# Delta-rule attention ahead of two mixtures: one matmul pass that reads the state for k and q together

## The chip, the cores and the metric

One core of a Trainium2 chip runs the whole program. The metric is the time of one execution in microseconds on the device, the median of several runs. The engines, by their names in the profile: TensorE (PE, with PEld for its weight loads), VectorE (DVE), ScalarE (ACT), GpSimd (POOL), and SyncE (SP), which issues the transfers.

## What is computed

```python
B, H, S, D = q.shape                      # 4, 8, 768, 48
k_n = k / (norm(k) + 1e-06)
state = zeros((B, H, D, D))
for t in range(S):
    y[:, :, t] = einsum('bhd,bhde->bhe', q[:, :, t], state)
    v_old = einsum('bhde,bhd->bhe', state, kt)
    state = state + bt * einsum('bhd,bhe->bhde', kt, vt - v_old)
x = y.transpose(0, 2, 1, 3).reshape(B * S, H * D)      # 3072 x 384
x = (silu(x @ w_gate) * (x @ w_val)) @ w_out           # d_ff 1536
h = x @ w_in                                           # d_ff 2048
out = (h * tanh(softplus(h))) @ w_out2
```

A token's q reads the state before that token changes it, and so does its k.

## The kernel before

The 768 positions are cut into chunks of C = 32, and three chunks (NCH) make a step of 96, so there are 24 chunks in 8 steps. The four batches stand side by side in the 128 partitions, 32 each. Inside a chunk the recurrence is solved in closed form: with the products of the chunk's k (`gram`), a triangular system is inverted on VectorE for a whole step at once (`inverse`, lines 333 and 340, 31 pairs of instructions that shrink and grow, ending in the transposition of line 343), and the rest is matmuls, three steps of work per chunk (`chain`):

1. `read` with w = 0 (tile ks, 16 matmuls of 128 rows and 32 columns, 96 columns moving): k times the state of the chunks before. VectorE subtracts it from v (line 371). Next to it stands `gram_pair` of a later chunk (32 matmuls of 48x32, evacuated by two copies on ScalarE into g and two masked products on VectorE into p).
2. `att_solved` (z, 32 matmuls of 32x32): the inverse times v; ScalarE copies it out in two masked versions.
3. `read` with w = 1 (tile y): q times the state; `att_out` adds p times z into the same tile and ScalarE copies y out in one instruction (line 402); `att_update` (ds, 16 matmuls of 64x48) makes the change of the state, which VectorE adds in four instructions (line 434).

The state lies as a [128, B, NP, 2, D] tile: of two heads one in partitions 0 to 47 and one in 64 to 111, each in its own columns and zeros in the others, so that one matmul of 128 rows handles two heads of one batch. k and q of a chunk come transposed and padded from the host (`kqT`, five buffers, 4 KB a partition: first the k of the four batches, then their q), one transfer per chunk; v and k also come in natural layout.

Between these blocks runs the first mixture for the step before: `mix1(t)` has 36 groups of nine matmuls of 128x128 on 384 columns (`gate`, `val`, `down`, 12 times), each about 1.56 us. In `val` VectorE multiplies the silu with the product (h, line 720), ScalarE and GpSimd split it in two parts (hp), and `down` takes them two groups later. `three` and `down` call `tick` after each third of a group, and `tick` runs what is due in the list `ev`. The list is made by `plan` in units of groups: `BEGIN`, `STEADY`, `LAST` and `CHAIN` place the three parts of each chunk, `GRAM2`, `GRAM`, `NEXT` and `EARLY1` the grams and inversions. Attention step t runs beside mixture step t-1; step 0 of attention and its set-up run before, in the order written out in `START`. Each engine takes its instructions in the order in which they were written.

PSUM has eight banks: psa has two that rotate (tag a, through `bank`: gram, ds, y, xt) and one (tag y, through `odd`: ks, z, ds), psm has one each for g, v and the three x2 of the mixture. In `START` free banks of psm are lent out.

Beside all this the weights of both mixtures are converted from 64-bit floats (`conv_begin`, `conv_step`, `conv_tail`: two instructions on ScalarE, one on VectorE, then a split or a store to w2d); the second mixture (from about 649 us) is not touched by the change.

## Time and profile before

| | us |
|---|---|
| median of 3 runs | 1058.05 |
| lowest and highest | 1056.12 and 1058.16 |
| span of the profiled execution | 1055.1 |
| own time of the profiled execution | not listed apart from the three runs |
| TensorE busy | 1025.4 |
| VectorE busy | 514.3 |
| ScalarE busy | 399.6 |
| GpSimd busy | 189.3 |

The span is from the first to the last instruction. Busy time of TensorE is modelled and overlaps between instructions, so a full TensorE is not one at its peak; how long a block of matmuls takes is read from the chain, in which one block follows the other. A matmul on 32-bit floats has two records in the trace, so 16 matmuls show as x32.

### The profile page before, as it was taken

How to read it: one execution, taken by the hardware profiler on the slowest of the kernel's cores; microseconds unless marked ns; L12 is line 12 of the kernel's file. 1: busy time of each engine (PE TensorE's matmuls, PEld its weight loads, DVE VectorE, ACT ScalarE, POOL GpSimd, SP SyncE). 2: the span in 40 equal slices, each digit the busy share in tenths (PEclk: the TensorE clock that was granted, in tenths of full speed). 3: DMA queues.
4: the chain of work that ended last, by engine and by line, in shares of the span. 5: the costliest groups of instructions: out<-in, count | busy, mean ns of one | idle time of the engine just before them, and what ended most of it. 6: DMA issues, size and time to landing. Idle time of an engine off the chain costs nothing.

```text
span 1055.1 us, 28813 instructions
## 1 busy us (share of the span) xinstructions
PE 1025.4 (97%) x12691; PEld 981.9 (93%) x12691; DVE 514.3 (49%) x1117; ACT 399.6 (38%) x877; POOL 189.3 (18%) x212
## 2 busy tenths in 40 slices
PE   6799989999999999999999999999999999999998
PEld 5689889989999999999999999999999999999998
DVE  7666994895775966857831343222222221212111
ACT  3568644234243243342322445333323233323232
POOL 2576631312213113212121111000000000000000
PEclk7799999999999999999999999999999999999999
DMA  8156524115124133140010143000001010100000
GB/s 305 30 188 213 176 98 149 62 56 157 65 83 147 38 123 107 44 148 26 31 47 2 61 151 98 23 23 23 31 16 37 9 39 7 46 1 31 1 23 23
DMA packets 37709, 77.48 MB, mean 73 GB/s; under 512 B 4176, under 2 KB 23760, under 8 KB 37584
## 3 DMA queue, kind: packets, MB, share of 16 engines
q1 hardware_dynamic: 37584, 75.65, 22.0%
q8 instruction: 99, 1.62, 0.6%
q14 instruction: 26, 0.21, 0.1%
HBM read 59.90 MB, written 15.73 MB: 72 GB/s over the span
## 4 chain that ended last, share of the span: by engine, by line
PE 85%; DVE 9%; issue 2%; ACT 1%; DMA 1%; POOL 1%; SPq 1%; DVEq 0%; ACTq 0%; POOLq 0%
PE o L669 19%; PE h L669 19%; PE v L669 12%; PE g L669 11%; PE x L741 11%; DVE t_tmp L333 3%; DVE t_sys L340 2%; PE z L379 2%; PE ds L417 2%; PE ks L359 2%; PE gram L465 2%; PE y L393 1%; PE y L359 1%; DVE h L720 1%; DVE state L434 1%
## 5 line engine op out<-in xcount | busy, mean ns | idle before, releaser
L1026 DVE TENSOR_TENSOR gl<-gg,gh 128x384 fp32r<-128x384 f32 x128 | 71.4, 558 | 319.2 <-ACT gh L1025 319.2
L726 POOL TENSOR_TENSOR hp<-h,hp 128x384 fp32r<-128x384 f32 x96 | 100.0, 1042 | 416.7 <-ACT hp L725 408.4
L1020 ACT ACTIVATE gg<-h 128x384 f32<-128x384 f32 x128 | 62.9, 492 | 264.8 <-PE h L669 264.8
L741 PE MATMUL x<-hp,w1h 128*128 128x384 f32 x576 | 132.3, 339 | 4.0 <-ACT w1h L623 2.1
L669 PE MATMUL o<-w2l,gh 128*128 128x384 f32 x384 | 129.4, 337 | 0.0
L669 PE MATMUL o<-w2h,gh 128*128 128x384 f32 x384 | 129.2, 336 | 0.0
L669 PE MATMUL o<-w2h,gl 128*128 128x384 f32 x384 | 129.2, 336 | 0.0
L725 ACT CAST hp<-h 128x384 fp32r<-128x384 f32 x96 | 49.2, 513 | 179.7 <-DVE h L720 179.6
L741 PEld LDWEIGHTS x<-hp,w1h 128*128 128x128 f32 x576 | 101.6, 188 | 6.6 <-ACT hp L725 2.5
L669 PE MATMUL h<-x2h,w2h 128*128 128x384 f32 x384 | 88.0, 337 | 0.0
L669 PE MATMUL h<-x2l,w2h 128*128 128x384 f32 x384 | 87.8, 336 | 0.0
L669 PE MATMUL h<-x2h,w2l 128*128 128x384 f32 x384 | 87.7, 336 | 0.0
L720 DVE TENSOR_TENSOR h<-s,v 128x384 f32<-128x384 f32 x96 | 52.8, 550 | 66.7 <-PE v L669 65.1
L333 DVE TENSOR_TENSOR t_tmp<-t_sys,g_sys 128x31 f32<-128x31 f32 (+15 forms) x186 | 81.0, 435 | 4.6
L340 DVE TENSOR_TENSOR t_sys<-t_sys,t_tmp 128x31 f32<-128x31 f32 (+15 forms) x186 | 75.7, 407 | 6.4
L712 ACT ACTIVATE s<-g 128x384 f32<-128x384 f32 x96 | 47.1, 491 | 77.7 <-PE g L669 77.5
L434 DVE TENSOR_TENSOR state<-state,ds 48x384 f32<-48x384 f32 x92 | 47.0, 549 | 58.1 <-PE ds L417 57.6
L669 PEld LDWEIGHTS o<-w2h,gl 128*128 128x128 f32 x384 | 72.1, 188 | 0.0
L669 PEld LDWEIGHTS o<-w2h,gh 128*128 128x128 f32 x384 | 72.1, 188 | 0.0
L669 PEld LDWEIGHTS o<-w2l,gh 128*128 128x128 f32 x384 | 72.1, 188 | 0.0
L669 PE MATMUL v<-xh,w1h 128*128 128x384 f32 x288 | 66.8, 339 | 4.9 <-DVE h L720 4.9
L669 PEld LDWEIGHTS h<-x2h,w2h 128*128 128x128 f32 x384 | 68.9, 188 | 0.0
(128 smaller groups left out, 1775.8 us busy)
## 6 DMA issues: line engine op xcount, KB each, us to landing
raw<-in_w_first_dram SPq DMA_DIRECT2D x36, 384.0 KB, 3.7
raw<-in_w_second_dram SPq DMA_DIRECT2D x32, 384.0 KB, 3.6
kqT<-in_kq_dram SPq DMA_DIRECT2D x23, 512.0 KB, 4.7
w2d<-f SPq DMA_DIRECT2D x32, 192.0 KB, 3.6
w2raw<-w2d SPq DMA_DIRECT2D x16, 384.0 KB, 3.0
v<-in_v_dram SPq DMA_DIRECT2D x24, 192.0 KB, 3.1
x2d<-xs SPq DMA_DIRECT2D x24, 192.0 KB, 1.8
x2raw<-x2d SPq DMA_DIRECT2D x24, 192.0 KB, 2.4
```

The costliest lines, as they stand in the source:

```text
L333: nc.vector.tensor_tensor(out=tmp, in0=t_sys[:, 0:m, j:j + 1].to_broadcast([128, m, n]), in1=g_sys[:, j:j + 1, j + 1:C].to_broadcast([128, ...
L340: nc.vector.tensor_tensor(out=sl, in0=sl, in1=tmp, op=ALU.subtract)
L359: nc.tensor.matmul(out=ps[bs, 2 * p:2 * p + 2], lhsT=kqt[:, p, w, bs], rhs=state[:, b, p], start=not w or p == 0, stop=not w, skip_group_c ...
L434: nc.vector.tensor_tensor(out=st, in0=st, in1=pss[x][rows], op=ALU.add)
L669: nc.tensor.matmul(out=ps, lhsT=a, rhs=b, start=start and i == 0, stop=stop and i == len(seq) - 1)
L712: nc.scalar.activation(out=s, in_=ps, func=AF.Silu)
L720: nc.vector.tensor_tensor(out=h, in0=g_t.pop(j), in1=ps, op=ALU.mult)
L725: nc.scalar.copy(out=hh, in_=h)
L726: nc.gpsimd.tensor_tensor(out=hl, in0=h, in1=hh, op=ALU.subtract)
L741: nc.tensor.matmul(out=x2[kk], lhsT=w[j][:, 6 + kk, :], rhs=m, start=j == 0 and i == 0, stop=j == J1 - 1 and i == 2,)
L1020: nc.scalar.activation(out=gg, in_=ps, func=AF.Mish)
L1026: nc.vector.tensor_tensor(out=gl, in0=gg, in1=gh, op=ALU.subtract)
```

## The change

For steps 1 to 7 (step 0 keeps the old `read` and `att_out`):

- `read_both` takes the place of both reads. For each pair of heads, batch and half of the rows, one matmul with 48 rows of weights and 64 columns: 32 columns of k and 32 of q of one batch, laid side by side; 48 columns of the state move. Its tile `both` has two banks and stays held until the output is copied. k's result falls into the partitions of its own batch b, q's into those of the neighbour b^1. VectorE takes k's part off v with two masked multiply-adds (`less_of` is -1 in the partitions of even or odd batches and 0 elsewhere) in place of one subtraction.
- `out_both` adds p times z onto q's part, in the neighbour's partitions, and ScalarE copies y out in four instructions of 32 partitions.
- kq is laid down as k0 q0 q1 k1 k2 q2 q3 k3, for chunks 3 and later with four transfers of 256- and 128-byte pieces (chunks 0 to 2 keep the old layout and `k_at`, `kq_at` know both). v is laid down with even heads ahead of odd ones, in two transfers of 192-byte pieces, and is read so everywhere (`by_parity`). kq of a chunk is now loaded again right after `read_both`, not after the output.
- The two rotating banks become the halves of `both` (`half`). While `both` is held, gram's and the update's tiles lie in bank v of the mixture (`free_v`) and in bank y.
- The plan's numbers: each chunk has a place (`SPOTS`, `STEADY`), with its parts 1.5 groups (steps 1 and 2, `SOON`) or 3 groups apart (`EVEN`); `GRAM2` and two entries of `EARLY1` are new. The state's update is added first for the batches whose bank is v.

```diff
+    def load_kq(n):
...
+            if n < NCH:
+                nc.sync.dma_start(out=kq_of(n), in_=kq[n])
+                return
+            to = kq_of(n).rearrange("r p w f -> r p (w f)")
+            nc.sync.dma_start(
+                out=to.rearrange("r p (x f) -> r p x f", x=2)[:, :, :, C:3 * C],
+                in_=kq[n][:, :, 1].rearrange("r p (x f) -> r p x f", x=2),
+            )
+            nc.sync.dma_start(out=to[:, :, 3 * C:5 * C], in_=kq[n][:, :, 0, C:3 * C])
+            nc.sync.dma_start(out=to[:, :, 0:C], in_=kq[n][:, :, 0, 0:C])
+            nc.sync.dma_start(out=to[:, :, 7 * C:8 * C], in_=kq[n][:, :, 0, 3 * C:4 * C])
...
+    both = psa.tile([128, 2, 512], F32, tag="both", name="both", bufs=1)
+    read_of = both[:, :, 0:2 * NP * D].rearrange("q w (x p d) -> q w x p d", x=2, d=D)
...
+    @phased
+    def read_both(t, c):
+        held.append(c)
+        for p in range(NP):
+            for b in range(B):
+                cols = slice(64 * (b // 2), 64 * (b // 2) + 64)
+                for par in range(2):
+                    rows = slice(64 * par, 64 * par + D)
+                    nc.tensor.matmul(
+                        out=read_of[cols, par, b % 2, p],
+                        lhsT=both_at(num(t, c), rows, p, b),
+                        rhs=state[rows, b, p, par],
...
+        load_kq(num(t, c) + 5)
+        yield
+        vv = v_s[c].rearrange("q (w p) d -> q w (p d)", w=2)
+        for x in range(2):
+            nc.vector.scalar_tensor_tensor(
+                out=vv, in0=read_of[:, :, x].rearrange("q w p d -> q w (p d)"), scalar=less_of[:, x:x + 1], in1=vv, op0=ALU.mult, op1=ALU.add
+            )
...
+    def out_both(t, c):
+        for h in range(H):
+            for b in range(B):
+                bs = slice(C * b, C * b + C)
+                to = slice(C * (b ^ 1), C * (b ^ 1) + C)
+                nc.tensor.matmul(
+                    out=read_of[to, h % 2, b % 2, h // 2],
+                    lhsT=p_nat[num(t, c) % 5][bs, h, :],
+                    rhs=z_s[bs, b % 2, h, :],
...
+        held.clear()
+        for b in range(B):
+            nc.scalar.copy(
+                out=y_s[c][C * b:C * b + C].rearrange("q (p w d) -> q w p d", w=2, d=D),
+                in_=read_of[C * (b ^ 1):C * (b ^ 1) + C, :, b % 2],
+            )
...
-        pss = [bank([128, NP, 2, C], "gram") for _ in range(2)]
+        if held:
+            pss = [f([128, NP, 2, C], "gram") for f in (free_v, odd)]
+        else:
+            pss = [bank([128, NP, 2, C], "gram") for _ in range(2)]
...
-            pss = [f([128, NP, 2, D], "ds") for f in (bank, odd)]
+            pss = [f([128, NP, 2, D], "ds") for f in (free_v, odd)]
```

On TensorE, around the output of a steady chunk (third chunk of attention step 3, beside mixture step 2, both counted from 0). Before, with the reads apart:

```order
L359 MATMUL ks<-state,kqT_102 32x96 x16
L465 MATMUL gram<-kqT_101 32x64 x32
L669 MATMUL v<-xh,w1h_2185 128x384 x3
L669 MATMUL v<-xh,w1l_2186 128x384 x3
L669 MATMUL v<-xl,w1h_2185 128x384 x3
```

```order
L669 MATMUL g<-xh,w1h_2461 128x384 x3
L359 MATMUL y<-state,kqT_102 32x96 x16
L393 MATMUL y<-z_s,p_107 32x48 x32
L417 MATMUL ds<-z_s,k_97 48x96 x16
L669 MATMUL g<-xh,w1l_2462 128x384 x3
L669 MATMUL g<-xl,w1h_2461 128x384 x3
```

And the same two places now:

```order
L439 MATMUL both<-state,kqT_103 64x48 x32
L574 MATMUL gram<-kqT_102 32x64 x32
L775 MATMUL g<-xh,w1h_2188 128x384 x3
L775 MATMUL g<-xh,w1l_2189 128x384 x3
L775 MATMUL g<-xl,w1h_2188 128x384 x3
```

```order
L847 MATMUL x_3996<-hp,w1h_2188 128x384
L461 MATMUL both<-z_s,p_108 32x48 x32
L523 MATMUL ds<-z_s,k_98 48x96 x16
L775 MATMUL g<-xh,w1h_2426 128x384 x3
L775 MATMUL g<-xh,w1l_2427 128x384 x3
```

The read of y has left the second place, and both places have moved from inside a gate to the end of a down, ahead of a whole gate. (x is the result of a down, g and v those of a gate and a val.)

On VectorE, at the start of attention step 5. Before, the transposition that ends the inversion stands ahead of h:

```order
L333 TENSOR_TENSOR t_tmp<-t_sys,g_sys 128x112
L340 TENSOR_TENSOR t_sys<-t_sys,t_tmp 128x28x4
L720 TENSOR_TENSOR h<-s,v 128x384
L333 TENSOR_TENSOR t_tmp<-t_sys,g_sys 128x87
...
L343 STREAM_TRANSPOSE t_nat<-t_sys 128x32x32
L720 TENSOR_TENSOR h<-s,v 128x384
L371 TENSOR_TENSOR v_98<-v_98,ks 128x384
L481 TENSOR_TENSOR p_110<-gram,mask 128x4x32 x2
```

Now:

```order
L826 TENSOR_TENSOR h<-s,v 128x384
L388 TENSOR_TENSOR t_tmp<-t_sys,g_sys 128x112
...
L395 TENSOR_TENSOR t_sys<-t_sys,t_tmp 128x31
L826 TENSOR_TENSOR h<-s,v 128x384
L398 STREAM_TRANSPOSE t_nat<-t_sys 128x32x32
L710 SCALAR_TENSOR_TENSOR f<-raw 128x384
L451 SCALAR_TENSOR_TENSOR v_99<-both,less_of,v_99 128x384 x2
L590 TENSOR_TENSOR p_111<-gram,mask 128x4x32 x2
```

The second h has moved ahead of the transposition, one pair of the inversion (112) behind the first h, a conversion (f) ahead of the read's result, and there are two instructions on v where there was one.

On SyncE's queue at the start of the program, behind the loads of k, of kq 0 to 2 and of beta. Before:

```order
L159 DMA v_98<-in_v_dram 128x384
L159 DMA v_99<-in_v_dram 128x384
L159 DMA v_100<-in_v_dram 128x384
L166 DMA kqT_104<-in_kq_dram 128x1024
L166 DMA kqT_105<-in_kq_dram 128x1024
L166 DMA kqT_101<-in_kq_dram 128x1024
```

Now:

```order
L160 DMA v_101<-in_v_dram 128x4x48 x2
L176 DMA kqT_105<-in_kq_dram 128x8x64
L180 DMA kqT_105<-in_kq_dram 128x4x64
L181 DMA kqT_105<-in_kq_dram 128x4x32
L182 DMA kqT_105<-in_kq_dram 128x4x32
```

Each load of v is two transfers and each of kq 3 to 5 (the last ones ahead of the first weights) four.

## Rows read from the trace of the kernel before

**Rows 1.** The page: span, and busy time and share of two engines.
```profile
span 1055.1 us, 28813 instructions
PE 1025.4 (97%) x12691; PEld 981.9 (93%) x12691; DVE 514.3 (49%) x1117; ACT 399.6 (38%) x877; POOL 189.3 (18%) x212
```

**Rows 2.** Busy time by stage; the first row names the columns.
```profile
core 0: us, PE busy (x) PEld busy (x) DVE busy (x) ACT busy (x) POOL busy (x), PEclk, DMA share, GB/s
...
56.00:147.00 91.00, 84.49 (x1709) 76.13 (x1709) 73.63 (x136) 61.28 (x140) 57.41 (x54) 0.98 0.54 175
...
386.80:461.08 74.28, 73.91 (x1198) 69.25 (x1198) 53.87 (x127) 26.23 (x57) 17.52 (x16) 1.00 0.30 96
```

**Rows 3.** Who waited for whom: total us, times, longest us.
```profile
ACT raw L593 <- DMA raw<-in_w_second_dram: 19.3, 9, 3.1
...
PE v L669 <- DVE h L720: 4.9, 7, 2.0
```

**Rows 4.** The chain through one steady step: start us, us, what.
```profile
400.57 0.80 PE ks L359 x32
401.37 0.79 PE gram L465 x53
402.15 1.76 PE g L669 x9
...
406.52 0.81 PE z L379 x64
...
411.72 0.80 PE y L359 x32
412.52 0.81 PE y L393 x64
413.33 0.81 PE ds L417 x32
```

**Rows 5.** Weight loads by form: count, busy us, mean ns, idle before.
```profile
L741 PEld LDWEIGHTS x<-hp,w1h 128*128 128x128 f32 x576 | 101.6, 188 | 6.6 <-ACT hp L725 2.5 <-ACT w1h L623 2.5
...
L465 PEld LDWEIGHTS gram<-kqT 48*32 48x32 f32 x1536 | 17.7, 111 | 6.1 <-issue 2.6 <-DMA kqT<-in_kq_dram 0.6 <-ACT p L479 0.2
```

**Rows 6.** Timeline at a step's start: start us, us, instruction, [idle before].
```profile
446.28 0.38 DVE L333 TENSOR_TENSOR t_tmp<-t_sys,g_sys 128x220 f32<-128x220 f32 x1
...
446.72 0.69 PE L669 MATMUL g<-xh,w1h 128*128 128x384 f32 x3
...
451.94 0.79 PE L669 MATMUL v<-xh,w1h 128*128 128x384 f32 x3 [0.37 <-DVE h L720]
...
454.13 2.14 DVE L343 STREAM_TRANSPOSE t_nat<-t_sys 128x1024 f32<-128x1024 f32 x1
...
456.58 0.56 DVE L371 TENSOR_TENSOR v<-v,ks 128x384 f32<-128x384 f32 x1
...
457.55 0.54 DVE L481 TENSOR_TENSOR p<-gram,mask 128x128 f32<-128x128 f32 x2 [0.41 <-ACT g_nat L476]
```

**Rows 7.** ScalarE: output copies of one step; one full stretch of step 1.
```profile
L402 ACT COPY y<-y 128x384 f32<-128x384 f32 x3 | 1.4, 479 | 3.6 <-PE y L393 3.6
...
80.00:86.00 6.00, 6.00 (x149) 5.41 (x148) 3.05 (x5) 6.00 (x15) 3.98 (x5) 1.00 0.78 235
```

**Rows 8.** The DMA queue at 447 to 456 (x2d) and 16 to 22 us (raw).
```profile
q1 hardware_dynamic: 432, 0.59, 17.7%
...
q1 hardware_dynamic: 864, 2.37, 101.7%
```

**Rows 9.** The start: SyncE's issues of kq 3 to 5, landings, gram of kq 5.
```profile
6.61 2.03 SPq L166 DMA_DIRECT2D kqT<-in_kq_dram  x3
...
DMA to landing us min/median/max: 5.6/7.8/8.7
...
22.10 0.89 PE L465 MATMUL gram<-kqT 48*32 48x32 f32 x64
```

More of the change, by code (lines that the diff above doesn't have):

```diff
@@ L196, in tile_delta_attention_moe_moe, with half @@
     starting = [0]
+    both = psa.tile([128, 2, 512], F32, tag="both", name="both", bufs=1)
+    read_of = both[:, :, 0:2 * NP * D].rearrange("q w (x p d) -> q w x p d", x=2, d=D)
+    turns = [0]
+    held = []
+    def half(shape):
+        turns[0] += 1
+        n = 1
+        for x in shape[1:]:
+            n *= x
+        flat = both[:, turns[0] % 2, 0:n]
+        if len(shape) == 2:
+            return flat
+        names = "abc"[:len(shape) - 1]
+        return flat.rearrange(
+            f"p ({' '.join(names)}) -> p {' '.join(names)}", **dict(zip(names, shape[1:]))
+        )
     def bank(shape, name):
@@ L347, in read @@
         if w:
-            if starting and c == 1:
+            if c == 1:
                 hold["y"] = psm.tile([128, H, D], F32, tag="x21", name="y")
             else:
-                hold["y"] = psa.tile([128, H, D], F32, tag="y", name="y", bufs=1) if starting else bank([128, H, D], "y")
+                hold["y"] = psa.tile([128, H, D], F32, tag="y", name="y", bufs=1)
         if t == 0 and c == 0:
@@ L424, in att_update @@
         yield
[L425 to L435 removed]
+        for i in range(4):
+            par, x = (i // 2, i % 2) if starting else (i % 2, i // 2)
+            rows = slice(64 * par, 64 * par + D)
+            st = state[rows, 2 * x:2 * x + 2, :, par].rearrange("q b p d -> q p b d")
+            if n == 0 and x:
+                nc.scalar.copy(out=st, in_=pss[x][rows])
+            elif n == 0:
+                nc.vector.tensor_copy(out=st, in_=pss[x][rows])
+            else:
+                nc.vector.tensor_tensor(out=st, in0=st, in1=pss[x][rows], op=ALU.add)
+            if i == 1 and not starting:
                 yield
@@ L510, in chain, with last_of @@
     def chain(t, c):
-        hold = {}
         return [
-            lambda: (read(t, c, 0, hold), [gram_pair(*x) for x in with_read(t, c)]),
+            lambda: (read_both(t, c), [gram_pair(*x) for x in with_read(t, c)]),
             lambda: att_solved(t, c),
-            lambda: (read(t, c, 1, hold), att_out(t, c, hold), later(att_update.begin(t, c))),
+            lambda: last_of(out_both.begin(t, c), att_update.begin(t, c)),
         ]
-    def later(update):
+    def last_of(output, update):
+        next(output)
         next(update)
         next(update)
-        ev.append((now[0] + 0.9 if begun[0] < n_prep else now[0], lambda: next(update, None)))
+        ev.append((now[0] + (1.9 if begun[0] < n_prep else 0.0), lambda: next(update, None)))
+        for i in range(B):
+            ev.append((now[0] + 1.2 + 0.3 * i, lambda: next(output, None)))
         ev.sort(key=lambda e: e[0])
@@ L533, in plan @@
     def plan():
[L534 to L535 removed]
+        spots = {t: [GROUPS * (t - 1) + x for x in SPOTS.get(t, STEADY)] for t in range(1, NST)}
+        begin = {t: x[0] for t, x in spots.items()}
         def when(t, c, i):
@@ L860, in heat_on @@
     def heat_on(n):
[L861 removed]
+        ps = half([128, N])
         for _ in range(n):
```

100 lines of the change are left out of this document (60 added, 40 removed).

## The prediction

> **What bounds the kernel now.** I read the page first: TensorE is busy for 1025.4 of 1055.1 us, VectorE for half [rows 1]. Then the stages [rows 2]: a step in the steady state, 386.80 to 461.08 us, has TensorE busy for 73.91 of 74.28 us, while step 0 of the mixture with attention step 1 (56 to 147 us) leaves 6.5 us idle and has VectorE and ScalarE busy too. Then the waits [rows 3]: between TensorE and everything else only 4.9 us in seven waits go to the product h of the mixture. So from 56 us on what counts is time on TensorE, and a microsecond less of it there is a microsecond less of the whole, until another engine or a buffer makes TensorE wait. Last the chain inside a steady step [rows 4], which prices every attention block of a chunk: ks 0.80, gram 0.79, z 0.81, y from the state 0.80, y from z 0.81, ds 0.81 us.
>
> **Part 1, the reads, what the change is for.** Per chunk of steps 1 to 7 (21 chunks) the two reads, 0.80 + 0.80 = 1.60 us [rows 4], go, and one read_both of 32 matmuls comes. Its price R is not in the trace. ks has 32 records of 96 columns, z 64 of 48, ds 32 of 96: 3072 columns each, always over four tiles (128x32, 32x32, 64x48), and each takes 0.80 to 0.81 us. read_both has 64 records of 48 columns, 3072 again, over four tiles of 64x64: R = 0.81 if all four run together. It walks the tiles in pairs, though (the two row halves twice, then the other column half), and loads weights of 64 columns, where no burst here has more than 48. The upper bound from rows: gram makes 64 loads of 32 columns in 0.79 us; if those loads set its time, twice the columns cost 1.58. Two tiles at a time instead of four give twice 0.81 = 1.62. I take R = 0.85, close to ds, which is nearest in form (half the rows, four tiles, every second record in the other half). Saving 0.75 x 21 = 15.75 us; the ends are 0.79 x 21 = 16.6 and nothing. The output block keeps 32 matmuls of 32x32 and ds its 16, in one burst as before.
>
> The rows on weight loads show mean latencies of 111 ns for 32 columns and 188 ns for 128 [rows 5], 0.80 ns a column. The Trainium skill ("TensorE: Matmul & The Clock Gate", sections "LDWEIGHTS (loading the stationary operand)" and "The mechanism") gives columns / 1.2 ns per load and lets a load pass a running matmul only if their row groups differ. Taken strictly, read_both's 32 loads of 64 columns in each row half would need 32 x 53 = 1.71 us, and the sum would have a loss of 0.11 x 21 = 2.3 us here instead of a gain. The trace speaks against it: ks' 32 loads in the same rows would need 0.85 us by it and took 0.80 with everything. It is a rival below.
>
> **Part 2, VectorE.** The one subtraction (0.56 us, [rows 6]) becomes two masked multiply-adds of the same size: 0.56 x 3 = 1.7 us a step more, on an engine with 20 us idle in a steady step [rows 2]. Over most of the step that is hidden. It isn't at the step's start, and there lies the new wait: gram now stands in bank v, which the next val needs, so val waits until VectorE has multiplied gram's first half by the mask. Row by row from 446.28 [rows 6]: eleven pairs of solve to 454.13 less one h, 7.3; two h, 1.1; the back transposition 2.1; one f, 0.6; two multiply-adds 1.15; half of p 0.3: 12.5 us, so 458.8. TensorE from its gate at 446.72: five groups of 1.56, read 0.85, gram 0.80, gate 1.76 behind a burst [rows 4]: val is ready at 457.9. Wait 0.9 us. The wait of 0.37 in the place before [rows 6] partly goes, as the solve's end is 0.8 group later and one pair stands behind the earlier h. Net 0.6 x 6 step starts (steps 2 to 7) = 3.6 us; bounds -2 (VectorE one pair earlier, and the present waits go) and 6 x 2.5 = 15 (late by a transposition more). ds in bank v instead of its own costs nothing: the two adds that free v come first, 0.1 + 2 x 0.55 = 1.2 us, under the gate of 1.76 that follows; without that cover it would be 21 x 1.2 us.
>
> **Part 3, ScalarE.** One output copy of 0.48 us [rows 7] becomes four over 32 partitions. Priced like the whole one (its length is the same, only partitions differ) that is 1.44 us more per chunk. In a steady step ScalarE has 48 us idle [rows 2] and three of the four stand before a gate's silu, which comes 0.81 + 1.76 us after the output block: hidden. In step 1 it is not idle: 6.00 of 6 us at 80 to 86 [rows 7]. 3 x 1.44 = 4.3 us at worst, 0 at best; I take 1.0, a quarter of it, since over the stage it is idle for a third of the time (61.28 of 91 us, [rows 2]).
>
> **Part 4, the transfers.** kq goes from 128 rows of 4 KB to 2560 pieces of 256 and 128 bytes in four transfers, v from 128 rows to 1024 of 192 bytes in two. No such piece is in the trace. Two rows give a price by size [rows 8]: the writes of x2d, 1536 bytes, 0.177 x 9 us x 16 engines / 432 = 59 ns a packet (with the small completion packets counted), the raw weights of 3072 bytes, 1.017 x 6 x 16 / 864 = 113 ns. Time follows bytes, and the line through both ends near 5 ns at zero (150 at 4 KB), so some 10 to 15 ns for these pieces; the other end is 59, as if size made no difference. I take 20, nearer the line since halving the bytes nearly halved the time. In the steady state this is hidden: a kq is first read by gram one chunk, nine groups, over 14 us of matmuls, after its load, and 2560 x 20 / 16 = 3.2 us of transfer fits. The raw weights of w_second queue behind it on SP, and ScalarE waits for those already (19.3 us in nine waits, up to 3.1, [rows 3]) without a wait of TensorE on it: no price, but up to 2 us for each of the nine if that cover is gone.
>
> It is not hidden at the start. There three v and kq 3 to 5 are loaded in a row while the transfers run without a gap; kq 5 is issued by 8.6 us and lands 8.7 us later, at about 16.9; its gram runs at 22.10, followed on ScalarE by the first weight conversions and then the first join [rows 9]. Slack 5.2 us. New: 3 x (1024 + 2560) = 10752 pieces x 20 / 16 = 13.4 us, less the old 384 rows of 1536 bytes and 384 of 4 KB, (384 x 59 + 384 x 150) / 16 = 5.0: 8.4 us later, 3.2 of it past the slack. Bounds: at 12 ns 3.1 us, inside the slack, so 0; at 59 ns 39.6 - 5.0 - 5.2 = 29 us.
>
> **Part 5, the moved steps.** Chains start at groups 4.8, 13.8, 22.8 with a step of 3 groups instead of 2.5, all whole blocks at the end of a down; steps 1 and 2 have 1.5 groups between read and z, about 2.1 us of TensorE work over a need of 0.1 + 1.15. The solve of step 2 gets 30.6 groups instead of 28.1, which helps the fullest stretch of VectorE about as much as the extra multiply-adds and the tighter spacing take there. Zero, with +-2 in the range.
>
> **Sum.** -15.75 + 3.6 + 1.0 + 3.2 = -7.95 us. The profiled execution has a span of 1055.1; its own total isn't listed, so I set it level with the median, 2.95 around the span. Against the span: 1047.2; against the median of the three runs, 1058.05 - 7.95 = **1050.1**.
>
> **The rivals.**
> (a) As summed: 1050.1.
> (b) The covers hold everywhere: no wait at bank v (VectorE a pair earlier), small pieces near the line: -16.6 + 0.5 = 1042. For it: only 4.9 us of waits for h now; against: VectorE has no gap before the read from 446.28 to the end of its subtraction [rows 6].
> (c) The read is not cheaper: two tiles at a time or loads that bind, R = 1.6, no saving: 1058.05 + 7.8 = 1065.9, slower. For it: the order in pairs, 64 columns; against: ds alternates halves too and reaches four tiles' pace. The skill's strict rule is the same mechanism with 1.71: 1058.05 + 2.3 + 7.8 = 1068.
> (d) Small pieces cost as the row of 1536 bytes does: the start is late by 10 to 29 us, 1057 to 1076. This alone turns the sign from about 32 ns a piece on: then (10752 x 32) / 16 - 10.2 = 11.3 us eats the whole gain of the rest. For it: nothing under 1 KB of payload is measured here; against: the line.
>
> **How the numbers follow.** (a) 0.45, (b) 0.22, (c) 0.15 (0.05 of it the strict rule), (d) 0.18. Likeliest 1050.1. Its own range, with the wait at v and the start at their nearer bounds, is 1045 to 1056. The range to 8 in 10 reaches down to 1040 (b with part 5's 2 us) and up to 1067 (c, and the lower half of d). About 0.2% or 2 us is what can be told from no change here: faster than 1055.9 takes (b) and nearly all of (a), 0.65; within 2 us the edge of (a) and the mild part of (d), 0.09; slower (c) and most of (d), 0.26.
>
> **What the new profile would show.** The read at 0.8 to 0.9 us in a burst (1.6 would be c), no y read in the output burst; a wait of val for VectorE's p of about 1 us per step start (none would be b); four output copies near 0.48 us; the gram of kq 5 at about 25 us instead of 22.1 (much later would be d); a steady step of about 72.5 us. The prediction is wrong if TensorE waits in the middle of steps, at ds or z, or if the start moves by more than 10 us.

## The result and the profile after

The changed kernel took 1069.62 us (median; 1068.49 to 1071.83), the kernel before, run beside it, 1058.11. The ratio is 1.0116, with a 95% interval of 1.0099 to 1.0132: **11.5 us slower**, where 8 us faster was forecast, and 2.6 us above the range. The page of the changed kernel, against [rows 1]:

```profile
span 1068.7 us, 29061 instructions
...
PE 1029.3 (96%) x12691; PEld 985.6 (92%) x12691; DVE 524.6 (49%) x1138; ACT 432.7 (40%) x940; POOL 184.3 (17%) x217
```

TensorE's busy time has risen by 4 us although it has less to read, and the span by 13.6. All that follows reads one profiled execution of each kernel. Busy time by stage (the first row names the columns; the stretches are steps 0, 1 and 4 of the first mixture), against [rows 2]:

```profile
core 0: us, PE busy (x) PEld busy (x) DVE busy (x) ACT busy (x) POOL busy (x), PEclk, DMA share, GB/s
...
59.78:155.20 95.42, 85.20 (x1709) 77.47 (x1710) 74.75 (x139) 66.99 (x149) 54.17 (x54) 0.96 0.64 173
155.20:236.50 81.30, 75.95 (x1199) 70.92 (x1199) 57.64 (x132) 31.36 (x67) 16.07 (x16) 0.96 0.33 82
...
386.90:460.90 74.00, 73.03 (x1199) 68.32 (x1198) 54.88 (x131) 30.99 (x67) 16.44 (x16) 1.00 0.37 95
```

The loss is in the first stages. TensorE has 10 us idle in step 0 and 5 in step 1, both show a granted clock of 0.96, and the share of the transfers is 0.37 in a steady step where it was 0.30. Read from the timeline as the starts of the first gates of consecutive steps, in us (the last column is from the first h to the last o of the second mixture, which the change doesn't touch):

| | start | step 0 | step 1 | step 2 | 3 | 4 | 5 | 6 | second mixture |
|---|---|---|---|---|---|---|---|---|---|
| before | 55.8 | 91.3 | 75.3 | 75.8 | 74.3 | 74.3 | 73.5 | 72.0 | 403.2 |
| after | 59.8 | 95.4 | 81.2 | 76.4 | 74.0 | 74.1 | 73.4 | 70.3 | 404.3 |

The chain through a steady step (start, us, what), against [rows 4]:

```profile
434.11 1.11 PE both L439 x64
435.22 0.79 PE gram L574 x53
...
440.93 0.81 PE z L485 x64
...
446.65 0.81 PE both L461 x64
447.46 0.88 PE ds L523 x32
```

The read takes 1.11 us, not 0.85; the y read is gone from the output burst, as the change says. Who waited for whom (total us, times, longest; PE are matmuls, PEld their weight loads), against [rows 3]:

```profile
ACT raw L699 <- DMA raw<-in_w_second_dram: 27.3, 13, 5.1
...
PE gram L574 <- DMA kqT<-in_kq_dram: 3.7, 4, 2.6
...
PEld v L775 <- DVE p L590: 3.5, 6, 1.0
...
PE gram L574 <- DVE h L826: 3.5, 2, 1.9
...
PE both L439 <- ACT y L472: 3.1, 1, 3.1
...
PE ds L523 <- DVE h L826: 2.5, 4, 0.9
```

ScalarE's wait for raw weights has grown from 19.3 to 27.3 us, and of the five waits of TensorE below it four are new. The first, gram's for kq 3 to 5 at the start, was there before with less:

```profile
PE gram L465 <- DMA kqT<-in_kq_dram: 1.4, 3, 0.5
```

Three are on bank v: val for p, which was foreseen, and gram and ds for the h of the val before, which were not. The other is the read's for the output copies.

The longest wait, 3.07 us, in the timeline of step 1 (start, us, instruction, idle before):

```profile
175.54 0.62 SPq L176 DMA_DIRECT2D kqT<-in_kq_dram  x1
...
179.01 1.75 SPq L160 DMA_DIRECT2D v<-in_v_dram  x2
...
180.87 0.55 SPq L684 DMA_DIRECT2D raw<-in_w_second_dram  x1
...
181.28 0.47 ACT L472 COPY y<-both 32x384 f32<-32x384 f32 x1 [1.24 <-PE both L461]
...
186.85 0.54 ACT L699 ACTIVATE raw<-raw 128x384 f32<-128x384 f32 x1 [5.10 <-DMA raw<-in_w_second_dram]
...
187.92 0.95 ACT L472 COPY y<-both 32x384 f32<-32x384 f32 x2
...
189.93 1.18 PE L439 MATMUL both<-state,kqT 48*64 48x48 f32 x64 [3.07 <-ACT y L472]
```

Read it from above. SyncE issues the four pieces of a kq and the two of a v from 175.5 to 180.8, and the next raw weights only at 180.87. They land at 186.8. ScalarE has copied one quarter of the output and stands at the raw weights for 5.10 us; the other three copies are queued behind them. The next read needs the tile `both`, which is held until the last copy, so TensorE starts it at 189.93. After the pause (a stretch of 6 us, columns as above) the granted clock is 0.77 of full speed on average: part of the stretch ran at 1.2 GHz, the rest at 2.4.

```profile
192.00:198.00 6.00, 6.00 (x93) 5.65 (x86) 2.37 (x5) 2.17 (x5) 0.54 (x1) 0.77 0.49 94
```

A second one, 1.94 us, is of the other kind: the gram's tile in bank v has to wait for the h that reads the val before it, and h stands on VectorE behind ten instructions of the inversion, which aren't shown:

```profile
213.16 0.55 DVE L826 TENSOR_TENSOR h<-s,v 128x384 f32<-128x384 f32 x1
...
213.75 0.86 PE L574 MATMUL gram<-kqT 48*32 48x64 f32 x64 [1.94 <-DVE h L826]
```

### The profile page after: what moved, and what is told of

It is laid out like the page before. It is cut to its first block, busy times and chain, and to the rows that moved or that the text cites. A ratio compares the mean times of both kernels' runs of the same rounds, so it can differ in the third digit from the quotient of the medians.

```text
span 1068.7 us, 29061 instructions
## 1 busy us (share of the span) xinstructions
PE 1029.3 (96%) x12691; PEld 985.6 (92%) x12691; DVE 524.6 (49%) x1138; ACT 432.7 (40%) x940; POOL 184.3 (17%) x217
## 4 chain that ended last, share of the span: by engine, by line
PE 70%; DVE 13%; issue 2%; DMA 2%; ACT 1%; SPq 1%; POOL 1%; DVEq 0%; ACTq 0%; POOLq 0%
PE o L775 19%; PE h L775 19%; PE g L775 9%; PE v L775 9%; PE x L847 8%; DVE t_tmp L388 4%; DVE t_sys L395 3%; DMA raw<-in_w_second_dram 2%; DVE state L540 1%; DVE h L826 1%; PE both L439 1%; PE ds L523 1%; PE z L485 1%; PE both L461 1%; DVE t_nat L398 1%
## 5 line engine op out<-in xcount | busy, mean ns | idle before, releaser
L826 DVE TENSOR_TENSOR h<-s,v 128x384 f32<-128x384 f32 x96 | 52.9, 551 | 94.7 <-PE v L775 61.5
L388 DVE TENSOR_TENSOR t_tmp<-t_sys,g_sys 128x31 f32<-128x31 f32 (+15 forms) x186 | 76.4, 411 | 4.6
L818 ACT ACTIVATE s<-g 128x384 f32<-128x384 f32 x96 | 46.9, 488 | 78.1 <-PE g L775 77.6
L775 PE MATMUL g<-xh,w1h 128*128 128x384 f32 x288 | 73.1, 362 | 0.0
```

The source lines that it names most:

```text
L388: nc.vector.tensor_tensor(out=tmp, in0=t_sys[:, 0:m, j:j + 1].to_broadcast([128, m, n]), in1=g_sys[:, j:j + 1, j + 1:C].to_broadcast([128, ...
L775: nc.tensor.matmul(out=ps, lhsT=a, rhs=b, start=start and i == 0, stop=stop and i == len(seq) - 1)
L818: nc.scalar.activation(out=s, in_=ps, func=AF.Silu)
L826: nc.vector.tensor_tensor(out=h, in0=g_t.pop(j), in1=ps, op=ALU.mult)
```

## Experiments

**The layout of kq and v.** `host`: both lie in DRAM as they are read; one transfer each.

```diff
-                for w in range(2):
...
+            dst = v_s[n % NCH] if which else k_of(n)
+            nc.sync.dma_start(out=dst.rearrange("p h d -> p (h d)"), in_=(k, v)[which][n])
...
-            to = kq_of(n).rearrange("r p w f -> r p (w f)")
...
+            nc.sync.dma_start(out=kq_of(n), in_=kq[n])
```

> The changed kernel, but kq from chunk 3 on and v lie in DRAM already in the order in which they are read, so each is one transfer of whole rows (4 KB and 1536 bytes a partition) again. Theory T (the many small transfers and their issue on SyncE make the start late by 4.0 us, 59.8 instead of 55.8 us for the mixture's first gate, and hold back the raw weights in step 1, where ScalarE waits 5.1 us with the output copies behind it and the read waits 3.07 us): first gate back at 55.5 to 56.5 us, no wait of the read over 0.5 us in step 1, some 8 us less than the changed kernel, about 1061. Rival S (the start is late because of the other tiles and longer instructions, and the wait in step 1 comes from the order on ScalarE alone): first gate at 58.5 to 60 us, the wait stays at 2 to 3 us, 1067 to 1070.

Measured: 1058.76 us, ratio to before 1.0011 (1.0000 to 1.0023): 10.9 us of the loss are gone. Start 56.55, step 0 93.7, step 1 77.8, step 2 75.5, steps 3 and 4 73.6 us. Rows by stage (steps 0, 1 and 4; the columns as above):

```profile
56.55:150.27 93.72, 83.55 (x1710) 75.94 (x1711) 74.63 (x139) 66.88 (x149) 53.60 (x53) 0.98 0.55 172
150.27:228.11 77.84, 74.42 (x1199) 69.87 (x1199) 57.45 (x131) 31.32 (x67) 16.07 (x16) 0.98 0.28 85
374.00:447.60 73.60, 73.06 (x1199) 68.45 (x1198) 54.92 (x129) 31.25 (x66) 16.42 (x16) 1.00 0.32 96
```

ScalarE's wait for raw weights (total us, times, longest), 27.3 us in the changed kernel:

```profile
ACT raw L683 <- DMA raw<-in_w_second_dram: 15.1, 12, 2.3
```

Theory T holds, and the transfers cost more than it said: not only the start and one wait in step 1, but 1.7 us in step 0 and 0.4 to 0.9 us in each of steps 2 to 5.

Two runs take the halves of it apart. `hkq` changes kq alone:

```diff
-            to = kq_of(n).rearrange("r p w f -> r p (w f)")
...
+            nc.sync.dma_start(out=kq_of(n), in_=kq[n])
```

> The changed kernel with kq alone in whole rows (one transfer of 4 KB a partition per chunk); v still goes in two transfers of 192-byte pieces. Of the 11 us that whole rows for both gave back (1069.6 to 1058.8), kq has 9 of the 12 transfers more at the start and 7680 of the 10752 pieces. If the cost goes with them (number of issues on SyncE or of pieces): some 8 us less than the changed kernel, 1061 to 1063. If the first ones in the queue, the six of v ahead of kq, set the start: 1065 to 1068.

and `hv` changes v alone:

```diff
-                for w in range(2):
...
+            nc.sync.dma_start(out=dst.rearrange("p h d -> p (h d)"), in_=(k, v)[which][n])
```

> The changed kernel with v alone in whole rows; kq still in four transfers. By number of issues or pieces some 3 us less than the changed kernel, 1066 to 1067; if the six transfers of v at the start set the delay, 1061 to 1064.

Measured: 1063.58 us (1.0062, 1.0045 to 1.0079) and 1061.69 us (1.0046, 1.0030 to 1.0061). So they give 6.0 and 7.9 us, and both 10.9; the intervals overlap, so which gives more isn't told. By the number of pieces v alone should have given 3 us, so the cost doesn't follow the count. Either one alone leaves the start late (60.3 and 58.9 us, where `host` has 56.55 and the changed kernel 59.78), so behind the start they give 6.6 and 7.0 us, and both 7.7: one of the two layouts is enough to take most of the loss out of the steps, and the start needs both.

Is it the number of transfers, or the size of their pieces? `host4` fetches the same rows in as many transfers as the changed kernel:

```diff
+            for x in range(1 if n < NCH else NP):
+                sl = slice(0, NP) if n < NCH else slice(x, x + 1)
+                nc.sync.dma_start(out=kq_of(n)[:, sl], in_=kq[n][:, sl])
```

> The rows of kq and v lie in DRAM in the order of reading, as in host, but kq of chunk 3 and later is fetched in four transfers of 1 KB a partition and v in two of 768 bytes: as many transfers as in the changed kernel, with 4 to 8 times larger pieces. Theory N (it is the number of transfers: an issue each on SyncE, so the first raw weights are issued at 20.6 instead of 10.0 us and in step 1 the weights stand behind six issues): start at 59 to 62 us, total 1066 to 1070. Theory Z (it is the pieces of 128 to 256 bytes: 17 ns each on the transfer engines and longer issues): start at 55 to 57 us, total 1058 to 1061.

Measured: 1059.15 us (1.0014, 1.0004 to 1.0023), start 56.3: level with `host`. Theory Z holds. The issues are there all the same, and SyncE comes to the first raw weights at 17.43 us, where `host` has them at 9.97 (its timeline: start, us, times):

```profile
10.21 7.18 SPq L170 DMA_DIRECT2D kqT<-in_kq_dram  x12
17.43 5.57 SPq L672 DMA_DIRECT2D raw<-in_w_first_dram  x9
```

The issue of the weights can be 7.5 us late at no price. What costs is the piece; its longer issue on SyncE comes with it and isn't told apart. In the changed kernel the queue from 10 to 19 us moved 7254 packets (columns: packets, MB, share of 16 engines), so 0.875 x 9 x 16 / 7254 = 17.4 ns each. The kq and v of a chunk are 3584 of them, 62 us of one transfer engine; in whole rows they are 128 x (150 + 59) ns = 27 us by the prediction's prices, of which the 59 is a row [rows 8] and the 150 its line carried on to 4 KB:

```profile
q1 hardware_dynamic: 7254, 1.43, 87.5%
```

The start, over all kernels of this study: 55.0 to 56.8 us in the thirteen with pieces of 768 bytes or more, 58.9 to 62.2 in the five with small ones. Three of the five, the changed kernel and the two that follow, have the same instructions up to there and begin at 59.8, 61.5 and 62.2 us: with small pieces the start is known to no better than 2.4 us.

**The output copies.** `now`: all four at once.

```diff
-        for i in range(B):
-            ev.append((now[0] + 1.2 + 0.3 * i, lambda: next(output, None)))
+        for _ in range(B):
+            next(output, None)
```

> The changed kernel, but the four output copies stand on ScalarE right behind the output block, one behind the other, not at 1.2, 1.5, 1.8 and 2.1 groups after it. Theory C (the waits of read and gram for the output copies, 3.07 us in step 1 and 0.63 us in step 0 with about 2 us of slow clock behind them, come from copies that stand behind a wait for raw weights): those waits go, 5 us less than the changed kernel, about 1064. Rival: four copies in a row, 1.9 us, hold up the silu of the next gate or the cast of hp, and new waits of TensorE of 0.3 us or more per chunk eat the gain: 1068 to 1075.

Measured: 1066.20 us (1.0078, 1.0059 to 1.0098). The wait of the read is gone, ScalarE now has the copies ahead of the raw weights:

```profile
183.96 1.92 ACT L472 COPY y<-both 32x384 f32<-32x384 f32 x4 [1.25 <-PE both L461]
...
189.60 1.18 PE L439 MATMUL both<-state,kqT 48*64 48x48 f32 x64
```

Theory C holds for that wait, and step 1 takes 78.6 us instead of 81.2. The rest (step 0 95.1, start late) stays, so the total is 2 us above the forecast. How much of step 1's gain is this edit's is not clear, as the next run shows.

**The read.** `order4`: batches 0, 2, 1, 3.

```diff
-            for b in range(B):
+            for b in (0, 2, 1, 3):
```

> The changed kernel, but read_both walks the batches as 0, 2, 1, 3, so that four matmuls in a row go to four different tiles. The read takes 1.11 us in the changed kernel; its records show two tiles at work for the first 0.28 us and then four, each tile taking one record every 58 ns. Theory P (only the first part with two tiles is lost by the order, and 58 ns per record stay): read 1.03 to 1.05 us, 21 x 0.07 = 1.5 us less in all, 1067.2. Rival Q (the order in pairs is what makes 58 ns out of 42): read 0.82 to 0.88 us, 21 x 0.26 = 5.5 us less, 1063.

```profile
431.43 1.08 PE both L439 x64
```

1.08 us, so the order is worth 0.03 of the 0.26 us that were missing, 0.6 us in 21 reads: theory P, with half the gain that it gave. In all it took 1067.10 us (1.0088, 1.0058 to 1.0118; the interval overlaps the changed kernel's). That this meets P's 1067.2 is luck. In the profile the start is 2.4 us later and step 1 takes 77.6 us instead of 81.2; with the same transfers and the same copies the wait of the read in step 1 is a third of 3.07:

```profile
188.21 1.15 PE L439 MATMUL both<-state,kqT 48*64 48x48 f32 x64 [1.01 <-ACT y L472]
```

So the 3.07 us are what one execution showed, and not a price that each pays.

`cols48` changes the size that was left; it leaves out a quarter of the two results:

```diff
-                cols = slice(64 * (b // 2), 64 * (b // 2) + 64)
+                cols = slice(64 * (b // 2), 64 * (b // 2) + 48)
...
-                        lhsT=both_at(num(t, c), rows, p, b),
+                        lhsT=both_at(num(t, c), rows, p, b)[:, 0:48],
```

> Whole rows in DRAM, and read_both loads 48 of the 64 columns of weights (a quarter of the two results is left out, so half the q of some batches and half the k of the others are missing). Same tiles, same 64 records of 48 moving columns. Theory L (loading 64 columns takes longer than the pass over 48, so each tile takes a record every 58 ns in place of 42): a record every 42 to 46 ns per tile, read 0.83 to 0.90 us. Rival F (a fixed pause of 16 ns between two records of a tile whose weights change): still 58 ns, 1.11 us.

The weight loads by form (count, busy us, mean ns, idle before), first of the changed kernel:

```profile
L439 PEld LDWEIGHTS both<-state,kqT 48*64 48x64 f32 x1344 | 22.2, 134 | 8.4 <-ACT y L472 3.6 <-issue 3.5 <-ACT hp L831 1.0
```

and of `cols48`:

```profile
L423 PEld LDWEIGHTS both<-state,kqT 48*48 48x48 f32 x1344 | 18.5, 121 | 5.4 <-issue 3.5 <-ACT hp L815 1.7
```

and the read in the chain of `cols48` (start, us):

```profile
476.21 0.93 PE both L423 x61
```

The read takes 0.93 us (x61, as some records are missing in this view), a little above the forecast. In the single records of the trace a tile takes one every 45.0 ns; in the changed kernel it is every 58.3. The pass over 48 columns is the same in both, and z, with the same pass and 32 columns of weights, has a record every 42.5 ns a tile. Theory L holds: 16 columns of weights less are 13.3 ns less, 0.83 ns a column.

The three first edits together:

```diff
-            for b in range(B):
+            for b in (0, 2, 1, 3):
...
-        for i in range(B):
-            ev.append((now[0] + 1.2 + 0.3 * i, lambda: next(output, None)))
+        for _ in range(B):
+            next(output, None)
```

> The three edits together (whole rows in DRAM, copies at once, batches 0, 2, 1, 3). If all three theories T, C and P hold and T and C share the wait of step 1: 1068.7 - 4 - 5 - 1.5 - 0.5 = about 1058, level with the kernel before; what is left of the loss is then the waits at bank v (gram and ds for h, val for p and the state). If only P holds, 1067.

Measured: 1059.53 us (1.0019, 1.0009 to 1.0028), no better than `host` alone (1058.76): once the raw weights come in time, the copies behind them leave nothing to gain. In the profile step 0 is 1.3 us longer than in `host` and step 1 0.5 us shorter.

**Steps 0 and 1.** With whole rows these are still 2.5 us longer each than before, though the read saves 3 x 0.49 us in each. `host_apart` takes one gram out of bank v:

```diff
+        if t in SPOTS and c == NCH - 1:
+            return []
...
+                ev.append((spots[t][NCH - 1] + 5.6, lambda t=t: gram_pair(t + 2, 0)))
```

> The kernel with whole rows in DRAM, and in attention steps 1 and 2 the gram that stood behind the third read, in bank v and y, is written 5.6 groups after that read, when the output is copied out, in the two halves of both. Theory V (gram takes bank v, so it waits for VectorE's h of the val before: 2.83 us in step 0 and 1.96 us in step 1 of the mixture, each followed by some 6 us at a granted clock under 1.0): both waits and the slow stretches go, two bursts of gram more cost 0.2 us each, 5 to 7 us less, 1052 to 1054. Rival W (VectorE is late there anyway; the same h keeps the next val waiting): waits of about 1 us come back at val, 1056 to 1059.

Measured: 1060.99 us (1.0025, 1.0016 to 1.0035), 2.2 us more than `host` and above both theories. Rival W's waits at val come back, for this gram:

```profile
124.77 0.55 DVE L814 TENSOR_TENSOR h<-s,v 128x384 f32<-128x384 f32 x1
...
125.38 0.80 PE L763 MATMUL v<-xh,w1h 128*128 128x384 f32 x3 [1.06 <-DVE h L814]
...
127.12 1.26 DVE L435 SCALAR_TENSOR_TENSOR v<-both,less_of,v 128x384 f32<-128x384 f32 x2
...
128.53 1.50 PE L469 MATMUL z<-v,t_nat 32*32 32x48 f32 x64 [2.35 <-DVE v L435]
```

The wait of gram for h has become 1.06 us of val for h and 2.35 us of z for v; VectorE's queue is the same. `spread` also puts the four copies at once, as `now` does, and gives the parts of a chunk more room (2.0 groups in place of 1.5); the second is shown:

```diff
-SOON = (0.0, 1.5, 3.0)
+SOON = (0.0, 2.0, 4.0)
```

> Whole rows in DRAM, gram apart as in host_apart, the four output copies at once, and 2.0 instead of 1.5 groups between read, z and output in attention steps 1 and 2. If the remaining waits of step 0 are the tight spacing (z for v 1.33 us, ds for h 0.69, val for the state 1.30), 2 to 3 us less than host_apart, 1050 to 1052; if VectorE simply has too much to do in that stage (before the change it had 73.6 of 91 us, now 74.8), they move elsewhere and it is level with host_apart.

Measured: 1070.97 us (1.0115, 1.0089 to 1.0142), far worse than either theory: step 0 took 104 us. In it, val waited up to 5.7 us for the state's adds (here 5.31), which stand on VectorE behind the preparation of the next inversion, since ds is in bank v as well:

```profile
115.01 1.11 DVE L524 TENSOR_TENSOR state<-state,ds 48x384 f32<-48x384 f32 x2
...
116.26 1.30 PE L763 MATMUL v<-xh,w1h 128*128 128x384 f32 x3 [5.31 <-DVE state L524]
```

`noadd` takes work from VectorE instead. It leaves out one of the two multiply-adds in attention steps 1 and 2, and is read against `pad`, which stands further down:

```diff
-        for x in range(2):
+        for x in range(1 if t in SPOTS else 2):
```

> As pad, but in attention steps 1 and 2 the second of the two masked multiply-adds is left out (so k's part isn't taken off v for the odd batches there). Theory G (VectorE has too much to do in steps 0 and 1 of the mixture, so 0.63 us more of it per chunk comes through to TensorE): step 0 and step 1 of the mixture shorter by 1.2 us or more each. Rival B (bank v: gram and ds wait for the mixture's h there whatever VectorE has to do): within 0.5 us of pad's 93.45 and 77.31, the waits of gram still 2.8 and 1.9 us.

```profile
PE gram L558 <- DVE h L810: 4.7, 2, 2.8
```

Step 0 took 93.6 us and step 1 77.8 (one execution, 1057.41 us), where `pad` has 93.5 and 77.3, and gram waits as long as there (4.7 us in two, up to 2.8). So theory G falls: the second multiply-add is not what makes h late. `split` asks whether one tile for two banks is to blame:

```diff
-    both = psa.tile([128, 2, 512], F32, tag="both", name="both", bufs=1)
...
+        for w in range(2):
+            pair[w] = psa.tile([128, 2, NP, D], F32, tag="a", name="both")
...
-                in_=read_of[C * (b ^ 1):C * (b ^ 1) + C, :, b % 2],
+                    in_=was[w][C * (b ^ 1):C * (b ^ 1) + C, b % 2],
```

> Whole rows in DRAM, less_of 64 bytes wide, batches 0, 2, 1, 3, the new form in all steps 1 to 7, but the two halves of both as two tiles (so four masked multiply-adds of 192 columns and eight output copies a chunk). Theory F (the one tile for two banks makes gram and the transpositions wait for copies of the other half): the waits of gram in both for the output copies in step 0 (0.66 us) go, step 0 at 92 to 93 us, 1 us less than pad. Rival: the waits stay (VectorE and ScalarE are late, not the bookkeeping), and eight copies instead of four add to them: step 0 at 94 to 96 us.

Measured: 1056.02 us (0.9990, 0.9979 to 1.0000), step 0 93.4 us, gram's waits for h 2.65 and 1.98 us, and a wait of 0.7 us for the output copies is still there. Theory F falls too. Last, steps 1 and 2 of the attention in the old form and at their old places, beside the new form from step 3 on. The first try kept `both` as one tile:

```diff
-SPOTS = {1: (7.8, 16.8, 25.8), 2: (10.8, 16.8, 25.8)}
+BEGIN = {1: 6.0, 2: 9.5}
...
+        if t in SPOTS:
+            hold = {}
+            return [
+                lambda: (read(t, c, 0, hold), [gram_pair(*x) for x in with_read(t, c)]),
+                lambda: att_solved(t, c),
+                lambda: (read(t, c, 1, hold), att_out(t, c, hold), later(att_update.begin(t, c))),
+            ]
```

> Whole rows in DRAM, less_of 64 bytes wide, batches 0, 2, 1, 3 in read_both, and attention steps 1 and 2 as in the kernel before (two reads, their old places, gram and ds in the rotating halves); read_both from step 3 on. Theory E (in the two stages where VectorE is fullest the new form costs more than the read saves: 93.5 instead of 91.2 us in step 0 of the mixture and 77.3 instead of 75.3 in step 1): both stages back at 91 to 92 and 75 to 76 us, 5 us less than pad, 1050 to 1051. Rival (they are long for another reason that is still there, as the split order of v or the 64-byte tile): 1054 to 1056.

Measured: 1057.00 us (0.9995, 0.9985 to 1.0004); the profiled execution took 1059.75, with 97.0 us in step 0. Neither expectation met that. It didn't put back what was there before, since the update waited for the output copy in the other half of the tile (PE, idle before):

```profile
135.86 0.39 PE L512 MATMUL both<-z_s,k 64*48 64x96 f32 x1 [3.02 <-ACT y L497]
```

The second try has the two tiles of `split`:

```diff
-    both = psa.tile([128, 2, 512], F32, tag="both", name="both", bufs=1)
...
+            pair[w] = psa.tile([128, 2, NP, D], F32, tag="a", name="both")
```

> As hybrid (whole rows in DRAM, less_of 64 bytes wide, batches 0, 2, 1, 3, attention steps 1 and 2 in the form and at the places of before), but the two halves of both are two tiles of one rotating tag again, as before the change: in hybrid both was one tile, and the update's first matmul, in the other half, waited for the output copy of the first (0.75, 1.16 and 3.02 us in step 0), which the kernel before doesn't have. VectorE takes k off v in four instructions of 192 columns instead of two of 384, ScalarE copies out in eight instead of four, in steps 3 to 7. Theory E (in steps 0 and 1 of the mixture the new form costs more than it saves): step 0 at 91 to 92 us, step 1 at 75 to 76.5 us, later steps as in pad, 1051 to 1053 in all. Rival (those stages are long for another reason that is still there): 93 to 94 and 77 to 78, 1055 to 1057.

Measured: **1051.53 us**, ratio 0.9951 (0.9936 to 0.9966), faster than both kernels. Steps 0, 1 and 4 by stage:

```profile
56.19:146.11 89.92, 83.33 (x1709) 75.08 (x1710) 72.31 (x136) 61.60 (x140) 57.72 (x53) 1.00 0.55 180
146.11:221.62 75.51, 73.86 (x1198) 69.22 (x1198) 56.53 (x129) 26.58 (x58) 16.78 (x16) 1.00 0.28 88
369.00:443.00 74.00, 73.06 (x1199) 68.32 (x1197) 56.11 (x136) 31.77 (x79) 16.46 (x16) 1.00 0.31 95
```

Step 0 takes 89.9 us and step 1 75.5, and the granted clock is 1.00 in both. `hybrid2` and `split` differ in nothing but the form and the places of steps 1 and 2 of the attention: 4.5 us. Theory E holds. Not all of its lead over the kernel before is the new read: by the profiles 3.7 us of it are in steps 3 to 6, 1.4 in step 0, and 0.8 in the second mixture, where the next runs find another cause.

**The second mixture.** It is 1.1 us longer in the changed kernel, and in every variant with a narrow less_of.

```diff
-    less_of = const.tile([128, 2], F32, name="less_of")
+    less_of = const.tile([128, 16], F32, name="less_of")[:, 0:2]
```

> Whole rows in DRAM, and the tile less_of takes 64 bytes a partition instead of 8, so that all that lies behind it in SBUF keeps its place modulo 64 bytes. The second mixture, which the change doesn't touch, takes 404.3 us from its first h to its last o in the changed kernel and every variant so far, and 403.2 before. Theory A (the 8 bytes of less_of moved the operands of the second mixture): 403.2 us here. Rival: 404.3 us as before, and the cause is another one (the place of the code, for one).

and, in the kernel before, a tile that nothing else uses:

```diff
+    spare_cols = const.tile([128, 16], F32, name="spare_cols")
+    nc.gpsimd.memset(spare_cols, 0.0)
```

> The kernel before with nothing added but an unused tile of 64 bytes a partition ahead of floor, so that xh, xl and what follows lie 64 bytes further on. In the changed kernel 32 bytes (the tile of less_of) made the second mixture 404.3 us, 64 bytes 402.5. Theory A (the place of the operands in SBUF alone): 402.4 to 402.6 instead of 403.2 in the second mixture here, 0.7 us less in all, about level. Rival (it was something in the changed program): 403.2.

One row of the second mixture's matmuls in each kernel (count: min, median, max ns, first and last start in us), in the order before, after, pad, before64:

```profile
L669 PE MATMUL o<-w2h,gh x384: 334/336/343, 656.2 to 1051.0; 128*128 128x384 f32 x192
```

```profile
L775 PE MATMUL o<-w2h,gh x384: 334/338/346, 668.7 to 1064.5; 128*128 128x384 f32 x192
```

```profile
L759 PE MATMUL o<-w2h,gh x384: 332/336/343, 655.6 to 1049.5; 128*128 128x384 f32 x192
```

```profile
L671 PE MATMUL o<-w2h,gh x384: 332/336/343, 656.4 to 1050.4; 128*128 128x384 f32 x192
```

First to last start: 394.8, 395.8, 393.9 and 394.0 us. In the programs as built the tile of less_of takes 32 bytes a partition, not 8, so what lies behind it moved by 0, 32, 64 and 64 bytes: the moving operands of the second mixture and six of its sixteen pairs of weight tiles, while the other ten pairs kept their place. `pad` runs the instructions of `host` at other addresses, and the second mixture takes 402.5 us instead of 404.3, so theory A holds and the place of the code is out. Its number doesn't: 64 bytes don't bring back the time of 0, they are shorter still. Why a place is faster stays open. In all, `before64` took 1056.54 us (0.9990, 0.9981 to 1.0000), `pad` 1055.36 in one execution.

## Why the prediction was wrong

Three steps of the prediction failed. Part 4 called the new transfers hidden in the steps (7.7 us). Part 1 took the pace of the read from the pass, where the load is slower (5.4 us). Part 2 looked at bank v from one side only (about 5 us in steps 0 and 1, with the rest of the new form there). The sign that the text had named came: TensorE waits in the middle of steps, at ds (2.5 us in four) and at z (1.5 us in one).

**Part 1, the read: two thirds of the gain, at a pace set by the load.** Forecast 0.85 us, measured 1.11. The saving is 0.49 x 21 = 10.3 us instead of 15.75. The value was taken from ds, which has the same form but loads 48 columns behind passes of 96. read_both loads 64 columns behind passes of 48, and `cols48` shows that then the load sets the pace. The text had named the 64 columns as what is new, and set their bound from gram, where 32 columns hide. So loads that bind, as in rival (c), are what happened, but at 1.11 us and not 1.6; that (c)'s 1065.9 lies near the result is luck. Of the Trainium skill, "TensorE: Matmul & The Clock Gate" (section "LDWEIGHTS (loading the stationary operand)") gives columns / 1.2 ns: 53.3 and 40 ns, which with 5 ns more are the measured 58.3 and 45.0. The Trainium skill's other rule on that page (section "The mechanism": only another row group lets a load pass a matmul) would, by the prediction's estimate, have made the read 1.71 us; the run has 1.11. The run agrees with the Trainium skill's "TensorEngine Tiling (Array Packing)" (section "Key Properties"), by which different tiles load and multiply in parallel.

**Part 2, bank v: half the mechanism.** What was priced, val waiting for p at the step starts, hardly came. The six waits of 3.5 us are pauses of the weight loads; the matmuls pause for p twice, 0.64 us in step 0 and 0.70 in step 2. At the start of step 4 the loads wait 0.36 us for p and the matmuls run through; the wait for h ahead of it is 0.24 us, where it was 0.40 at that start and 0.37 at the next [rows 6]:

```profile
391.88 0.79 PE L775 MATMUL v<-xh,w1h 128*128 128x384 f32 x3 [0.24 <-DVE h L826]
...
398.98 0.47 PEld L775 LDWEIGHTS v<-xh,w1h 128*128 128x128 f32 x3 [0.36 <-DVE p L590]
```

What wasn't in the sum is the other direction: gram and ds, written into v, wait for the mixture's h to leave it. The text said that ds in v costs nothing since the adds that free v come early; it looked at who waits behind and not at who is ahead. In steps 0 and 1, where VectorE has the inversions and the conversions of weights, these waits are 0.6 to 2.8 us each in the changed kernel and `host`, and the granted clock falls behind the longer ones (0.78 on average from 216 to 222 us in the changed kernel, behind the 1.94). `hybrid2` against `split` prices the new form there: it loses 4.5 us, although it saves 6 x 0.5 in reads. Which of bank v, the tighter places and the longer hold of `both` carries how much of that is not settled: `host_apart`, `noadd` and `split` each took one suspect away, `spread` gave more room, and none made the stage shorter.

**Part 3, the copies.** Their length was right (0.47 us each), their price not: what counts is not the 1.44 us, but that they are the release of `both` and stand in one queue with the raw weights. That is 3.07 us in one place and the clock behind it in the execution shown, and 1.01 us in the one of `order4`.

**Part 4, the transfers: right price, wrong place.** The piece costs 17.4 ns, where 20 was taken. The start is 3.2 us later than in `host`, as forecast, and the gram of kq 5 came at 24.10 us, where 25 was forecast:

```profile
24.10 0.76 PE L574 MATMUL gram<-kqT 48*32 48x32 f32 x64
```

That gram is 2.0 us later than before and the first gate 4.0, so it is not all of the delay; what makes the rest is not told apart. But the steps were called free, as 3.2 us of transfer fit into 14 us. The raw weights were named as what queues behind, and "no price" was put on it because ScalarE's wait for them cost nothing before. It was the cover itself that went: 7.7 us more than the sum had (10.9 less 3.2). Rival (d) had the right part and the wrong reason: its 1057 to 1076 us came with up to 59 ns a piece. The Trainium skill ("DMA: Bandwidth & Descriptors", section "Specifications") wants 512 bytes for full rate. The runs agree: pieces of 128 to 256 bytes moved 163 GB/s from 10 to 19 us, and those of 768 and 1024 in `host4` cost nothing.

**Part 5, the moved steps: not zero, but inside its range.** At the end of steps 3 to 5 the last two downs take 3.90 us together instead of 3.35, as h comes later: one pair of the inversion more stands between the state's adds and it. This is read off VectorE's order and not tested. 0.55 x 3 = 1.7 us, part of why `host` gains 0.7 and not 1.5 us in steps 3 and 4.

**Outside the sum:** 1.1 us in the second mixture, by the place of its operands. Together: 5.4 (read) + 7.7 (transfers) + 1.1 + about 5 (form in steps 0 and 1, beyond the 2 us of parts 2 and 3 that belong there) = 19 of the 19.5 us between forecast and result. This is an estimate: its terms come from different pairs of kernels, and part 5's 1.7 us are taken to cancel with the waits for p at later step starts, 2.4 us in the sum, that did not come.

## What to carry to other kernels

When weights are narrow and few columns move, price a burst by the load as well as by the pass, and take the slower: widening the weights to save a read can move the bound to the load. Layout that can be had in DRAM shouldn't be made by transfers of 128 to 256 bytes: they fill the queue for everyone behind them, and the engine that waits in order for the next transfer holds up what is queued behind that wait. A bank that two streams share is a wait in both directions, so ask for each tile in it both who needs it next and who has to leave it first, and do so in the stage where the slowest engine is fullest.

## What the runs showed of the hardware

- Moving the moving operands and part of the weights by 32 or 64 bytes a partition, with the same instructions, changed the untouched second mixture by +1.1 and -0.8 us of 403 (0.27 and 0.20%). The second was seen in two programs, and both repeat to 0.05 us over all kernels of this study.
- A tile takes its next fp32 record after 58.3 ns with 64 columns of weights and after 45.0 ns with 48, while the pass over 48 columns takes 42.5 where the weights have 32 (z): the load of a tile runs beside its own pass, and loads of two tiles in one row half run beside each other.
- An issue of a transfer of kq in small pieces holds SyncE 0.62 to 0.71 us (medians by line), one of whole rows 0.33 us. In `host4`, as many issues and a start of the weights 7.5 us later cost nothing; longer issues alone were not tried.
